# Rebuilding the order of all engines' instructions with measured times of small operations, in a four-layer attention kernel

## The chip, the cores and the metric

One NeuronCore of a Trainium2 chip. The metric is the device time of one execution in microseconds (us). Where a ratio is given, it is the mean time of one kernel's fast runs over the mean of the other's fast runs of the same rounds, with a 95% interval; it is therefore not quite the ratio of the medians that stand beside it.

## The reference, cut to what matters

Four residual layers on a sequence of 2048 rows of 512, 32 heads of 16:

```python
x = A_x
x = x + _A_ref(_layernorm(x), A_wqkv, A_w_phi, A_wo)   # linear attention
x = x + _B_ref(_layernorm(x), B_wqkv, B_wo)            # windowed attention
x = x + _A_ref(_layernorm(x), A_wqkv, A_w_phi, A_wo)
x = x + _B_ref(_layernorm(x), B_wqkv, B_wo)
# A: phi = softmax(q @ w_phi), softmax(-q @ w_phi); kv = sum over ALL rows of phi_k v; o = phi_q kv / (phi_q z)
# B: each row attends to rows i, i-2, ..., i-14 of its own head
```

The sum over all rows in A is what divides the run: nothing of A's output can start before all four row blocks have given their part. These are the two barriers of the text.

## The kernel before

The kernel is written as work items in threads ("stage.engine"). A list of 1452 entries replays them in one global order, so this list sets the order in which the instructions of all five engines stand in the program. Two more tables go with it: for each of 383 copies, residual adds and the like, whether Vector or Scalar does it, and for each buffer that is taken, which slot it gets.

```python
    def slot(self, kind):                       # which buffer
        k = self.ntile[kind]
        self.ntile[kind] = k + 1
        return kind + _SLOTS[kind][k]
    # ... cut ...
    def flex(self, stage, fn, *args):           # Vector ("1") or Scalar
        k = self.nflex
        self.nflex += 1
        self.step(stage, "F%d%s" % (k, fn.__name__), fn, *args, _CHOICE[k] == "1")
    # ... cut ...
    def run(self):
        self.setup()
        self.stages()                           # makes the threads
        n, left = {}, None
        for w in _ORDER.split():                # replays them
            key = self.names[int(w, 36)]
            i = n.get(key, 0)
            n[key] = i + 1
            self.threads[key][i]()
            if key == "flag.DVE" and i == 1:
                left = _OPT["flag_lag"]         # 12: the flag is read 12 entries later
            if left is not None:
                left -= 1
                if left == 0:
                    self.redo = self.flag()     # all engines read the flag (safe path or not)
        # ... cut ...
```

## Time and profile before

| | before |
|---|---|
| time, median of 3 | 333.4 us (332.74, 333.40, 334.26) |
| time of the profiled execution | 331.28 us (span in the trace 329.5) |
| busy Tensor, Vector, Scalar | 311.5, 302.7, 279.2 us |
| start to barrier 1, barrier 1 to 2, to the end of the last windowed product, from there to the end | 52.6, 157.2, 110.1, 9.6 us |

The lines behind the busy times are in the prediction. Barrier 1 is the start of the first `kvT` copy, barrier 2 the start of the second layer pair's `ZM` product, in all tables below.

### The profile page before, as it was taken

To read this page: it belongs to the slowest core of one execution; us is meant where nothing else is said; L and a number is where in the kernel's file an instruction comes from. 1 tells how busy PE (TensorE), PEld (TensorE's weight loads), DVE (VectorE), ACT (ScalarE), POOL (GpSimd) and SP (SyncE) were. 2 spreads that over 40 slices of the span, in tenths; PEclk is the share of its full clock that TensorE was granted. 3 is DMA by queue.
4 is the path that set the end of the run, shared out by engine and by line. 5 is a ranking of instruction groups with operands and counts; after the bars stand their busy time and mean duration, and the time that the engine had idled before them with its cause. 6 is when DMAs were issued, how large, how long until landed. Compare 5 with 4: busy or idle time off the path is not lost.

```text
span 329.5 us, 8061 instructions
## 1 busy us (share of the span) xinstructions
PE 311.5 (95%) x3203; PEld 149.7 (45%) x3203; DVE 302.7 (92%) x443; ACT 279.2 (85%) x634; POOL 26.9 (8%) x50
## 2 busy tenths in 40 slices
PE   8999999999999999899999999789999999997892
PEld 3645456435444454344443464543554444442330
DVE  8999994988999999899999999699999999999992
ACT  4999997999988979799999999699997887766550
POOL 4000000000040004000000000000004042400000
PEclk9999999999999999999999999999999999999998
DMA  7990000013757699994670300023359969799733
GB/s 200 313 252 6 0 2 4 2 47 92 127 141 152 143 156 138 139 157 98 114 148 4 64 3 2 4 69 90 116 72 190 133 130 147 138 150 160 161 115 120
DMA packets 37389, 35.42 MB, mean 107 GB/s; under 512 B 23008, under 2 KB 32224, under 8 KB 37344
## 3 DMA queue, kind: packets, MB, share of 16 engines
q1 hardware_dynamic: 36816, 34.81, 54.4%
q8 instruction: 27, 0.44, 0.7%
q14 instruction: 18, 0.15, 0.2%
q10 hardware_dynamic: 528, 0.02, 0.1%
HBM read 10.50 MB, written 2.36 MB: 39 GB/s over the span
## 4 chain that ended last, share of the span: by engine, by line
PE 60%; ACT 13%; DMA 12%; DVE 7%; SPq 3%; issue 2%; ACTq 0%; DVEq 0%
PE ps L893 18%; PE ps L516 9%; DMA Vg<-V 7%; PE ps L601 6%; PE ps L589 6%; PE ps L694 5%; DMA xnT<-xn 4%; PE ps L981 3%; ACT Ek L595 3%; ACT Eq L702 3%; PE ps L1045 2%; SPq L945 2%; DVE Eq L812 2%; PE ps L456 2%; ACT sqd L536 2%
## 5 line engine op out<-in xcount | busy, mean ns | idle before, releaser
L893 PE MATMUL ps<-xnT,WB 128*128 128x512 bf16 x384 | 88.4, 380 | 0.8 <-DMA xnT<-xn 0.8
L1036 DVE TENSOR_TENSOR pav<-PT,Vg 128x4096 bf16<-128x4096 bf16 (+1 forms) x34 | 71.8, 2162 | 1.9 <-DMA Vg<-V 1.2
L974 DVE TENSOR_TENSOR prod<-QT,K 128x4096 bf16<-128x4096 bf16 x32 | 72.2, 2285 | 0.5 <-ACT K L189 0.3
L893 PEld LDWEIGHTS <-WB 128*128 128x128 bf16 x384 | 42.3, 114 | 44.1 <-issue 7.6
L516 PEld LDWEIGHTS <-oT 128*128 128x128 bf16 x256 | 23.6, 98 | 33.6 <-ACT oT L189 4.3
L189 ACT CAST oT<-ps 128x512 bf16<-128x512 f32 (+1 forms) x55 | 29.5, 584 | 8.1 <-PE ps L1045 7.7
L702 ACT ACTIVATE Eq<-ps 128x512 bf16<-128x512 f32 x64 | 34.6, 617 | 1.3 <-PE ps L694 1.3
L595 ACT ACTIVATE Ek<-ps 128x512 bf16<-128x512 f32 x64 | 33.8, 612 | 0.8 <-PE ps L589 0.8
L516 PE MATMUL ps<-WoB,oT 128*128 128x512 bf16 x128 | 32.8, 380 | 0.3 <-ACT oT L189 0.2
L516 PE MATMUL ps<-WoA,oT 128*128 128x512 bf16 x128 | 30.9, 380 | 0.8 <-DVE oT L187 0.8
L694 PE MATMUL ps<-xnT,WA 128*128 128x512 bf16 x128 | 31.3, 380 | 0.2 <-DVE Eq L812 0.2
L536 ACT ACTIVATE sqd<-x 128x512 bf16<-128x512 bf16 x48 | 29.9, 629 | 1.3 <-DVE x L529 1.1
L601 PE MATMUL ps<-WA,xnT 128*128 128x512 bf16 x128 | 30.6, 379 | 0.0
L589 PE MATMUL ps<-WA,xnT 128*128 128x512 bf16 x128 | 30.4, 379 | 0.0
L529 DVE SCALAR_TENSOR_TENSOR x<-ps,x 128x512 bf16<-128x512 f32 x38 | 24.9, 684 | 1.4 <-PE ps L516 1.3
L189 ACT CAST K<-ps 128x512 bf16<-128x512 f32 x32 | 18.7, 591 | 3.6 <-PE ps L893 3.3
L189 ACT CAST QT<-ps 128x512 bf16<-128x512 f32 x31 | 18.2, 600 | 3.0 <-PE ps L893 3.0
L1045 PE MATMUL ps<-pav,indAV 128*32 128x512 bf16 (+1 forms) x272 | 17.5, 370 | 3.3 <-DVE pav L1036 2.9
L935 POOL COPY vh<-V 128x64 bf16<-128x64 bf16 x6 | 7.5, 1244 | 161.7 <-ACT V L189 161.7
L526 ACT ACTIVATE x<-ps 128x512 bf16<-128x512 f32 x26 | 15.1, 593 | 6.2 <-PE ps L519 5.7
L601 PEld LDWEIGHTS <-xnT 128*128 128x128 bf16 x128 | 12.3, 98 | 14.7 <-issue 0.4
L589 PEld LDWEIGHTS <-xnT 128*128 128x128 bf16 x128 | 12.3, 98 | 14.6 <-ACT xnT L189 0.4
(127 smaller groups left out, 451.1 us busy)
## 6 DMA issues: line engine op xcount, KB each, us to landing
Vg<-V SPq DMA_DIRECT2D x128, 131.5 KB, 4.5
Prho<-rd SPq DMA_DIRECT2D x8, 512.0 KB
x<-in_A_x_dram SPq DMA_DIRECT2D x3, 512.0 KB, 7.2
WB<-in_B_wqkv_dram SPq DMA_DIRECT2D x3, 512.0 KB, 8.9
wraw<-in_A_wqkv_dram SPq DMA_DIRECT2D x4, 256.0 KB, 4.5
out_dram<-x SPq DMA_DIRECT2D x4, 256.0 KB, 2.2
out_dram<-x SPq DMA_DIRECT2D x8, 128.0 KB, 2.5
x<-in_A_x_dram SPq DMA_DIRECT2D x4, 128.0 KB
```

Source lines behind the costliest of these rows:

```text
L189: self.nc.scalar.copy(out=out, in_=in_)
L516: nc.tensor.matmul(y[:], lhsT=oT[:, c, t * P:(t + 1) * P], rhs=Wo()[:, c, :], start=(c == 0), stop=(c == NB - 1 and not onpe))
L529: nc.vector.scalar_tensor_tensor(out=xb[:, t, :], in0=T[t][:], scalar=1.0, in1=xb[:, t, :], op0=ALU.mult, op1=ALU.add, **kw)
L536: nc.scalar.activation(out=sqd[:], in_=xb[:, t, :], func=ACT.Square, accum_out=T["ss"][:, t:t + 1])
L589: nc.tensor.matmul(pk[:], lhsT=xnT[:, t, k, :], rhs=self.WA[:, k, D:2 * D], start=(k == 0), stop=(k == NB - 1))
L595: nc.scalar.activation(out=T["E"][:, t, s, :], in_=T["k", t][:], func=ACT.Exp, scale=1.0 - 2.0 * s)
L601: nc.tensor.matmul(pv[:], lhsT=xnT[:, t, k, :], rhs=self.WA[:, k, 2 * D:3 * D], start=(k == 0), stop=(k == NB - 1))
L694: nc.tensor.matmul(pq[:], lhsT=self.WA[:, k, hb * P:(hb + 1) * P], rhs=xnT[:, :, k, :], start=(k == 0), stop=(k == NB - 1))
L702: nc.scalar.activation(out=self.Eq[L, b][s][:, :, hb, :], in_=T[hb][:].rearrange("p (t i) -> p t i", t=4), func=ACT.Exp, scale=1.0 - 2.0 * s)
L893: nc.tensor.matmul(pp[:], lhsT=self.WB[:, k, i * D + c:(i + 1) * D:NB], rhs=xnT[:, :, k, :], start=(k == 0), stop=(k == NB - 1))
L974: nc.vector.tensor_tensor(out=pr[:], in0=QT[:, c:c + 1, :].to_broadcast([P, NW, TB]), in1=win, op=ALU.mult)
L1036: nc.vector.tensor_tensor(out=pv, in0=PT[:, :, lo:lo + n].unsqueeze(1).to_broadcast([P, NB, 2, n]), in1=vw, op=ALU.mult)
```

## The change

Its intent: the three tables are planned anew, now with the measured times of small Vector and Scalar operations. New options come in as well, all off. Only the tables differ in what is emitted; core of the diff:

```diff
 _ORDER = """
-9 d6 b6 8 e a c 0 0 d i i i 0 0 i i i f h i i i i i i i i g j k o p j l 3 1x 1y t 3 1x t u m b o q r 34 1z s t
+av 8 i i i i i i i i i i i i 0 f 0 g e 2t 0 bs 9 h a d c 0 j k t i i j l 27 o p 3 3 d6 b 1x 1x t 1y o m 2 2 1q
 ... (all 1452 entries in a new order)
 _CHOICE = ( ... )     (86 of 383 flipped)
 _SLOTS = { ... }      (all four kinds new)
+    "v_dram": (), "half_mo": (), "rho_pad": 0,      (in the options; off, their code emits what was emitted)
```

## The prediction

> **What bounds the kernel now.** I read four views of the kernel before, in this order: the busy line of the page, the groups by line, Vector's waits in stretches of time, and the timelines of Tensor and Vector about the places where both lose time.
>
> The busy line and the slices, page parts 1 and 2 (busy tenths in 40 slices of 8.2 us):
>
> ```profile
> PE 311.5 (95%) x3203; PEld 149.7 (45%) x3203; DVE 302.7 (92%) x443; ACT 279.2 (85%) x634; POOL 26.9 (8%) x50
> ...
> PE   8999999999999999899999999789999999997892
> DVE  8999994988999999899999999699999999999992
> ```
>
> Three engines are nearly full at once. The span is 329.5 us, so Vector has 26.8 us in which it does nothing (329.5 - 302.7), and that includes the first 2 us and the end. It dips at slices 6 and 7 (about 50 to 57 us) and at slice 25 (about 206 to 214 us). These are the two barriers: the sums over keys of an A layer need all four row blocks, and nothing of the attention output can start before. Between row blocks, layers overlap, so there is other work at every other time.
>
> The costliest groups (line, engine, operation, shapes, count | busy us, mean ns | idle before):
>
> ```profile
> L893 PE MATMUL ps<-xnT,WB 128*128 128x512 bf16 x384 | 88.4, 380 | 0.8 <-DMA xnT<-xn 0.8
> L1036 DVE TENSOR_TENSOR pav<-PT,Vg 128x4096 bf16<-128x4096 bf16 (+1 forms) x34 | 71.8, 2162 | 1.9 <-DMA Vg<-V 1.2
> L974 DVE TENSOR_TENSOR prod<-QT,K 128x4096 bf16<-128x4096 bf16 x32 | 72.2, 2285 | 0.5 <-ACT K L189 0.3
> ```
>
> 144 of Vector's 302.7 us are 66 large products of the windowed layer that no order can shorten, and the idle time before them is 2.4 us in all. Little is lost inside the big work.
>
> Vector's named waits, from the list of waits of the whole run (us in total, times, longest):
>
> ```profile
> DVE ZM L749 <- PE ps L740: 2.4, 2, 1.8
> DVE kvT L187 <- PE ps L664: 2.0, 1, 2.0
> DVE rho L797 <- ACT Ds L793: 1.6, 2, 0.8
> DVE pav L1036 <- DMA Vg<-V: 1.2, 1, 1.2
> ```
>
> The first three are the two barriers and the short chain of small operations behind each. The largest other named wait is 1.2 us. So there is no single hole for a new order to fill.
>
> Tensor's timeline just before the first barrier:
>
> ```profile
> 50.49 2.04 PE L664 MATMUL ps<-Ek,vaug 128*33 128x64 bf16 x128
> 52.47 1.04 PE L694 MATMUL ps<-xnT,WA 128*128 128x512 bf16 x4
> ```
>
> From 7.2 to 52.5 us the chain that ended last is Tensor nearly without a break. Four matmuls of 512 columns take 0.86 us there, 215 ns each, against the 380 ns that the page gives as the duration of one: starts overlap, so I count Tensor by 215 ns. Priced so, Tensor has 20.1 us of issue in 20 to 40 us and 20.1 in 40 to 60: full. In 120 to 140 it has 17.1, in 200 to 220 it has 15.2, and in 300 to 329.5 about 18. So **Tensor bounds the start up to the first barrier**, Vector, Scalar and Tensor take turns between the barriers, and **Vector bounds the last 100 us** (20.00 of 20 us busy in 280 to 300).
>
> **What the Trainium skill says.** "VectorE: DVE Perf Modes", section "The TRN2 errata", gives (N+151)/0.96 ns for a Vector tensor_tensor at one element a cycle: 161 ns for 4 elements, 691 for 512. The trace agrees: 157 to 163 ns for the 128x4 statistics, 684 for the residual adds. The same table gives Scalar 224 cycles plus one an element at 1.2 GHz: 190 ns for 4 elements, and the trace has 206 for the 128x4 Exp but 296 for the 128x4 Ln; here the measurement decides. So small operations are nearly all fixed cost, and a planner that takes them for free is off by 0.2 to 0.3 us at each. "Perfetto Trace Analysis", section "Identifying the Most-Contended Engine", says that matmul busy share is no measure of nearness to the roofline; the 380 against 215 ns above agrees, and is why I do not read 95% as 5% of slack. Its section "Optimization Strategy" advises to go by regimes and to look for the gaps on the engine that binds in each; that is how I split the sum.
>
> **The change part by part.** The new options (values through memory, split output product, a padded row) are off, so their code emits what was emitted before. What differs is the order list, the choice of Vector or Scalar for 383 copies, residual adds and the like, and the slots of the buffers. The listing of the built programs shows the same number of instructions for Tensor, DMA issue and GpSimd. No product is made smaller.
>
> Of the choices, 86 flip. Pricing them by the groups (copy of 128x512 out of PSUM: Vector 0.686, Scalar 0.60; layer-norm apply: 0.408 and 0.808; 128x1024 transposed copy: 0.682 and 1.03; residual with its accumulator: 0.77 and 0.68; a product that reads PSUM itself 0.680, or 0.416 behind a Scalar copy of 0.60):
> - before the first barrier, to Vector: 3 applies, 3 transposed copies, 2 others; to Scalar: 2 applies, 7 copies. Vector -1.24 us, Scalar -0.08.
> - the rest of the first two layers: Vector +0.59, Scalar -1.33.
> - the last two layers: Vector -0.48, Scalar +1.13.
> - sum: Vector -1.1 us of 302.7, Scalar -0.3 of 279.2, Tensor 0.
>
> What of it lies on the path:
> 1. Start to first barrier: Tensor is full and its list before the barrier holds the same units in both (the transpose of the sums is at the same place). The 1.24 us that Vector saves become a longer wait, 0 us gained. Some Tensor units trade places, +-0.5.
> 2. First barrier to second: Scalar carries the chain in about 140 to 149 and 188 to 206 us, and loses 1.33 us of work; Vector gains 0.59. I credit half of the difference, -0.4 us. Of about 6 us of Vector's idle time here I let a better plan take a fifth, -1.2. This fifth is a choice; nothing in the listing proves it.
> 3. Second barrier: before, both late copies of V stood ahead of the last normalization (206.78 us). Now one stands behind it on Vector, 0.69 us, and the last key sums need it. +0.4.
> 4. Second barrier to the end: Vector-bound, -0.48 us of work, counted whole: -0.5. The lists of the last 20 us end alike (last product in halves, two projections, two residual adds, stores), so the 10 us from the last Vector product (ends 319.8) to the end stay: 0.
> Sum: -1.7 us. From 333.4 that is 331.7; I put **331.5**, since the order was presumably kept for looking better to its planner.
>
> **The rivals.**
> - *The better plan pays fully.* If right prices let the planner close half of Vector's removable idle time (26.8 less about 2 at the start and 8 at the end, so 17) the gain is 8 us, 325 us. For it: many small operations, 48 accumulator reads of 197 ns on Scalar alone. Against: the largest single wait outside the barriers is 1.2 us, and idle time at barriers is a chain of latencies, not order.
> - *Order moves the wait.* The windowed layer waits for gathered V at 126 to 135 us, with the DMA engines at 1.06 of their share in 120 to 140. The order of those transfers is unchanged in the first two layers, so saved Vector time ahead of it would only lengthen that wait. In the last two layers one more of row block 2's four gathers now stands behind those of row block 3; if it is late, Vector idles up to one landing time, 4.5 us (the page's median). That would make 334 to 337.
> - *Scalar becomes the bound in 222 to 260 us*, where it has 18.7 and 17.5 of 20 us and takes 1.13 us more. It would cancel step 4: 332 to 333.
>
> **Range and chances.** The planned terms sum to a couple of us. Errors: about 2 us from the idle time that I guessed in step 2, 1.5 from steps 1 and 3, 1 from spread of runs (before: 332.74 to 334.26). Together about 3: 8 in 10 between 327.5 and 335.0. Faster by over 2% means under 326.7, a gain of 6.7 us, 40% of the removable idle time: 0.08. Slower by over 2% means over 340: 0.03. Within 2%: 0.89.
>
> **What would show it right or wrong.** Step 1: the end of the first key sums stays within 0.7 us of 52.5, and Vector's wait for it is longer than 2.0 us. Step 2: Vector's idle time from 62 us to the second barrier falls by 1 to 2 us. Step 3: the second barrier's kvT evacuation comes within 2 us of 208.7, with the wait for it not shorter. Step 4: from there to the end 120.8 us becomes about 120. Busy sums: Vector 301.6, Scalar 279, Tensor issue unchanged. It is wrong if a wait for gathered V of over 2 us shows up on Vector, if Tensor stalls before the first barrier, or if the idle time between the barriers shrinks by 4 us or more.

## More of the kernel before

In four of the A layers' eight row blocks (2 and 3 of each layer) the reciprocal sums `rho` go through memory, so that they come back spread over all partitions; Vector multiplies the features by what comes back:

```python
        def wr():
            # ... cut ...
            nc.sync.dma_start(out=dst, in_=T["rho"][:])
        def rdb(s):                              # s = 0, 1: two reads of 512 KB
            T["P", s] = pr = self.med([4, NB, P], "Prho")
            # ... cut ...
            nc.sync.dma_start(out=pr[:].rearrange("p t a i -> p (t a i)"), in_=src)
        def muld(s):                             # Vector's product with it
            ev = self.Eq[L, b][s]
            nc.vector.tensor_tensor(out=ev[:], in0=ev[:], in1=T["P", s][:], op=ALU.mult)
```

And the output of a layer, whose residual add is a choice too:

```python
        def res(t, onpe):                        # "1": Tensor adds by an identity matmul, Scalar evacuates
            # ... cut ...
            if onpe:
                nc.scalar.activation(out=xb[:, t, :], in_=T[t][:], func=ACT.Identity, **kw)
            else:                                # "0": Vector adds
                nc.vector.scalar_tensor_tensor(out=xb[:, t, :], in0=T[t][:], scalar=1.0, in1=xb[:, t, :], ...)
        # ... cut ...
        def store(lo, hi):
            ov = self.out.rearrange("b (j p) d -> p (b j) d", p=P)
            nc.sync.dma_start(out=ov[:, 4 * b + lo:4 * b + hi, :], in_=xb[:, lo:hi, :])
```

## The result, and the profile after

| | before | after |
|---|---|---|
| time, median of 4 each | 333.07 us (332.54 to 334.26) | 329.17 us (328.77 to 330.32) |
| ratio of the means | | 0.9884 [0.9846, 0.9921] |
| busy Tensor, Vector, Scalar | 311.5, 302.7, 279.2 | 310.3, 302.2, 279.3 |

The time lies in the range and in the class that was given the best chance (within 2%), but the gain is 3.9 us and 1.7 had been added up. Run again in five rounds (controls below) it was 2.8 us, 0.9915 [0.9888, 0.9943].

The page of the kernel after, parts 1 and 2 (busy times; busy tenths in 40 slices):

```profile
PE 310.3 (95%) x3176; PEld 149.5 (46%) x3203; DVE 302.2 (92%) x439; ACT 279.3 (85%) x634; POOL 25.3 (8%) x50
...
PE   7999999999999999999999999979999999999873
...
DVE  7998995998998999899999999699999999999993
```

The busy times hardly move; the dips at the barriers stay. So most of what was gained is idle time: Vector's is 26.8 us before (329.5 - 302.7) and 25.3 after (327.5 - 302.2). Vector's named waits in the kernel after (us in total, times, longest):

```profile
DVE ZM L753 <- PE ps L744: 2.4, 2, 1.9
...
DVE rho L801 <- ACT Ds L797: 1.6, 2, 0.8
...
DVE pav L1081 <- DMA Vg<-V: 1.0, 1, 1.0
...
DVE kvT L190 <- PE ps L668: 0.7, 1, 0.7
```

The barrier waits are as before, but for the one at barrier 1 (2.0 before, 0.7 after), and no wait for gathered V has grown. To find where the gain is, the run was cut in four at the same events in each trace. Columns of this view are: stretch and length, then busy time (and instructions) of Tensor, weight load, Vector, Scalar, GpSimd, then clock, DMA share, GB/s. The kernel before, from its start to barrier 1, from 9.4 us after barrier 1 to barrier 2, from there to the last windowed product, and the tail:

```profile
0.00:52.58 52.58, 51.12 (x584) 28.20 (x585) 47.81 (x105) 46.60 (x97) 5.21 (x30) 1.00 0.44 122
62.00:209.81 147.81, 145.55 (x1459) 69.29 (x1458) 138.27 (x187) 137.10 (x321) 8.11 (x11) 1.00 0.54 96
209.81:319.91 110.10, 102.96 (x982) 46.76 (x983) 106.37 (x125) 86.85 (x199) 13.58 (x9) 1.00 0.68 121
319.91:329.50 9.59, 3.17 (x22) 1.18 (x20) 3.29 (x12) 0.61 (x2) 0.00 (x0) 0.84 0.46 149
```

The kernel after, the same stretches:

```profile
0.00:52.44 52.44, 50.36 (x579) 28.11 (x585) 47.04 (x104) 46.30 (x98) 5.12 (x30) 1.00 0.42 122
61.90:209.28 147.38, 145.02 (x1447) 68.94 (x1459) 139.16 (x188) 136.70 (x320) 7.27 (x11) 1.00 0.56 97
209.28:318.93 109.65, 102.56 (x973) 46.86 (x982) 106.14 (x126) 87.30 (x199) 12.91 (x9) 1.00 0.65 126
318.93:327.50 8.57, 3.23 (x22) 1.03 (x19) 3.04 (x7) 0.49 (x2) 0.00 (x0) 0.94 0.31 103
```

In this pair of traces the largest part (1.0 us of 2.0) is the tail, to which the prediction had given zero; between the barriers 0.4 us. But the pair explains 2.0 us and the timed runs differ by 3.9, so the profile of the kernel before is hardly of a usual run. That is what the experiments had to find out.

### The profile page after: what moved, and what is told of

It is laid out like the page before. It is cut to its first block, busy times and chain, and to the rows that moved or that the text cites. A ratio compares the mean times of both kernels' runs of the same rounds, so it can differ in the third digit from the quotient of the medians.

```text
span 327.5 us, 8033 instructions
## 1 busy us (share of the span) xinstructions
PE 310.3 (95%) x3176; PEld 149.5 (46%) x3203; DVE 302.2 (92%) x439; ACT 279.3 (85%) x634; POOL 25.3 (8%) x50
## 5 line engine op out<-in xcount | busy, mean ns | idle before, releaser
L192 ACT CAST oT<-ps 128x512 bf16<-128x512 f32 (+1 forms) x60 | 32.1, 587 | 8.4 <-PE ps L1090 7.1
L605 PE MATMUL ps<-WA,xnT 128*128 128x512 bf16 x120 | 30.0, 380 | 0.5 <-issue 0.2
L593 PE MATMUL ps<-WA,xnT 128*128 128x512 bf16 x124 | 29.7, 380 | 0.6 <-DMA xnT<-xn 0.2
L520 PE MATMUL ps<-WoA,oT 128*128 128x512 bf16 x120 | 29.2, 380 | 0.4
L192 ACT CAST V<-ps 128x512 bf16<-128x512 f32 x31 | 17.5, 595 | 4.4 <-PE ps L927 4.3
L192 ACT CAST K<-ps 128x512 bf16<-128x512 f32 x31 | 17.8, 585 | 3.7 <-PE ps L927 3.3
L192 ACT CAST QT<-ps 128x512 bf16<-128x512 f32 x29 | 17.1, 592 | 2.5 <-PE ps L927 2.5
L651 DVE TENSOR_TENSOR Ek<-Ek,rk 128x4096 bf16<-128x4096 bf16 (+1 forms) x10 | 18.6, 1858 | 0.5 <-ACT rk L646 0.5
L593 PEld LDWEIGHTS <-xnT 128*128 128x128 bf16 x128 | 12.1, 97 | 15.4 <-DMA xnT<-xn 0.7
L446 ACT ACTIVATE xn<-x,nmr,rstd 128x512 bf16<-128x512 bf16 x23 | 18.2, 822 | 1.0 <-DVE nmr L435 0.8
```

The costliest lines, as they stand in the source:

```text
L192: self.nc.scalar.copy(out=out, in_=in_)
L520: nc.tensor.matmul(y[:], lhsT=oT[:, c, t * P:(t + 1) * P], rhs=Wo()[:, c, :], start=(c == 0), stop=(c == NB - 1 and not onpe))
L593: nc.tensor.matmul(pk[:], lhsT=xnT[:, t, k, :], rhs=self.WA[:, k, D:2 * D], start=(k == 0), stop=(k == NB - 1))
L605: nc.tensor.matmul(pv[:], lhsT=xnT[:, t, k, :], rhs=self.WA[:, k, 2 * D:3 * D], start=(k == 0), stop=(k == NB - 1))
```

## The experiments

The record marks all variants as correct; even the one that is wrong on purpose passed the check. Twelve kernels ran, three calls of four, each on one chip with eleven runs of the kernel before; each kernel was run six times. By the author's account, five more variants did not build: the list with an item moved and the old slot table deadlocks, since a slot is then asked for before its holder is done. The traces' stretches, in us:

| kernel (first half / second half of the list) | to barrier 1 | barrier 1 to 2 | to last product | tail |
|---|---|---|---|---|
| before (profiled execution 331.28) | 52.58 | 157.23 | 110.10 | 9.59 |
| control of before (333.02) | 53.35 | 158.82 | 109.60 | 9.43 |
| after (329.18) | 52.44 | 156.84 | 109.65 | 8.57 |
| control of after (330.05) | 53.32 | 156.87 | 109.64 | 8.47 |
| after / before, cut at barrier 2 (331.90) | 53.11 | 156.70 | 111.14 | 9.15 |
| before / after, cut at barrier 2 (332.74) | 53.78 | 158.79 | 109.64 | 8.79 |
| before, one store earlier (332.56) | 52.83 | 158.92 | 109.85 | 9.20 |
| before, other factor in one product | 52.97 | 157.22 | 109.29 | 9.22 |
| after, one store later | 52.39 | 157.05 | 109.64 | 9.42 |

### Controls and grafts: which half carries it

The two kernels again under new names, and two grafts. At entry 985 of both lists, which is barrier 2, the same items have been done, so the lists can be joined there:

```diff
-order, choices, slots of one kernel
+first 985 entries of one kernel, the rest of the other; choices and slots go with their items
```

> The kernel before itself, run as a null control. Both theories: ratio 1.000 within 0.4%. It also gives a second trace: if the last Vector product again ends near 319.9 us and the span near 329.5 us, the profiled run of before was typical; the timed runs (332.5 to 334.3) against the profiled one (331.3) suggest instead a span of 330.5 to 332 us.

> The changed kernel again, for a tight size of the effect. Expected 0.988, interval within 0.984 to 0.992. Its trace should repeat: second barrier (first ZM product) at 209.3 us, last Vector product ended at 318.9, last residual add at 322.9, span 327.5.

> Changed order, choices and slots up to the second barrier, where both orders have done exactly the same work, and those of before from there on. Theory 1 (the gain comes late: Vector-bound second half and the tail; the traces show the second barrier only 0.5 us earlier): gain of 0.3 to 1.2 us, ratio 0.996 to 0.999. Theory 2 (the gain comes from the first two layers, and the profiled run of before was lucky there): ratio about 0.990 to 0.993, with the second barrier 2 us or more before that of the control.

> Order, choices and slots of before up to the second barrier, the changed ones from there on. Theory 1: most of the gain, ratio 0.989 to 0.994, the span after the second barrier 118.2 us as in the changed kernel (before 119.7). Theory 2: ratio 0.996 to 1.000.

| | median, us (lowest to highest) | ratio to before |
|---|---|---|
| control of before | 332.30 (330.59 to 333.30) | 0.998 [0.9947, 1.0013] |
| control of after | 329.81 (329.05 to 330.53) | 0.9915 [0.9888, 0.9943] |
| after, then before (graft_AB) | 330.79 (329.94 to 331.90) | 0.9943 [0.9915, 0.9970] |
| before, then after (graft_BA) | 330.92 (329.43 to 332.74) | 0.9942 [0.9912, 0.9971] |
| before, 11 runs | 332.82 (330.78 to 333.37) | |

Each half by itself gains about 0.6%, the whole 0.85%: neither carries it all, and the intervals are too wide to divide it. So neither theory held alone: the graft with the new first half reached barrier 2 2.4 us before the control (209.81 and 212.17 us), as theory 2 had it, and the other one kept about two thirds of the gain, just outside theory 1's range. (The profiled execution of the latter is the slowest of its six; its trace is only 0.2 us shorter than the control's, so most of its gain is not in that trace. The graft with the old second half is 1.3 us longer to its last product than the other traces of that half, 111.14 against 109.3 to 110.1, so a part of what it lacks may be the seam.) The start is the same for all (52.4 to 53.8 with no regard to the list), so by the traces the first half's part lies between the barriers, and the second half's is mostly the tail. Between the barriers the stretch takes two values with the old list, 157.2 and 158.8, and one with the new, 156.7 to 156.9. The control of before shows what the first profile did not. Vector's timeline of that control near 96 us (start, duration, line, operation, tiles; in brackets the idle time ahead of it and what ended it):

```profile
96.31 1.22 DVE L829 TENSOR_TENSOR Eq<-Eq,Prho 128x2048 bf16<-128x2048 bf16 x1
97.77 0.16 DVE L431 SCALAR_TENSOR_TENSOR nmr<-sums,rstd 128x4 f32<-128x4 f32 x1 [0.24 <-ACT rstd L427]
97.97 0.41 DVE L440 TENSOR_SCALAR xn<-x,rstd,nmr 128x512 bf16<-128x512 bf16 x1
100.34 1.23 DVE L829 TENSOR_TENSOR Eq<-Eq,Prho 128x2048 bf16<-128x2048 bf16 x1 [1.95 <-DMA Prho<-rd]
```

Vector stands 1.95 us for the second read of rho, that of row block 3 (counted from 0) of the first A layer; two of the expectations name the block or the layer wrongly. In the first profile of before this product ran at 97.40 us without a wait. With the old first half, three of four traces have the wait (1.95, 1.97, and 1.14 with another 1.10 beside it in the graft); the three that have it were executions of 332.56 to 333.02 us, the one without took 331.28. The timed runs of before fall into the same two groups: of 33, eight are at 331.62 or below and 25 at 331.94 or above, a gap of only 0.3 us between the groups. With the new first half no trace has it:

```profile
96.03 2.39 DVE L835 TENSOR_TENSOR Eq<-Eq,Prho 128x2048 bf16<-128x2048 bf16 x2
98.33 0.15 DVE L435 SCALAR_TENSOR_TENSOR nmr<-sums,rstd 128x4 f32<-128x4 f32 x1
```

Here (kernel after) both products run one behind the other. How the read is issued shows in Sync's queue of transfers (SPq: start and duration of the issue; `xnT` is a layer's transposed input, `Vg` the V that is gathered for the windowed layer). The control of before:

```profile
84.51 0.57 SPq L825 DMA_DIRECT2D Prho<-rd  x1
85.85 4.40 SPq L447 DMA_TRANSPOSE xnT<-xn  x1
90.35 0.60 SPq L825 DMA_DIRECT2D Prho<-rd  x1
94.50 8.39 SPq L945 DMA_DIRECT2D Vg<-V  x8
```

The kernel after:

```profile
83.10 0.57 SPq L831 DMA_DIRECT2D Prho<-rd  x1
87.06 3.03 SPq L451 DMA_TRANSPOSE xnT<-xn  x1
90.19 0.60 SPq L831 DMA_DIRECT2D Prho<-rd  x1
95.28 6.79 SPq L988 DMA_DIRECT2D Vg<-V  x8
```

In both the second read stands behind a transpose. The difference shows in the records of single packets, which tell rho reads (4096 B), transposes (256 B) and gathers (4208 B) apart:

```
                     read 1          transpose (bulk)  read 2          product starts
before               85.10 -  88.89   88.53 -  90.91   90.86 -  95.58    97.40
control of before    85.87 -  89.82   89.48 -  92.93   91.73 -  99.39   100.34
before, store moved  85.34 -  89.34   89.03 -  92.43   91.26 -  98.88    99.85
before / after       86.30 -  90.38   90.15 -  93.61   92.37 -  99.95   100.8
after                84.45 -  88.44   88.35 -  91.03   91.57 -  95.59    97.2
control of after     85.35 -  89.30   89.22 -  91.92   92.31 -  96.33    98.1
```

With the old list the second read starts before the transpose is through. In the three bad traces the two overlap for 1.2 us, but hardly move in it: the last 15 to 29 of the transpose's 2048 packets start there and 11 to 14 of the read's 128. The rest of the read follows, takes 7.6 us in all in place of 4.7, and its end falls among the gathers of V. With the new list the transpose is issued later (4.0 us after the first read in the kernel after, 1.3 us in the control of before), its issue is shorter (3.03 against 4.4 us), the read starts 0.4 to 0.5 us after the transpose has ended and takes 4.0 us in each trace. The lists agree with this: the transpose stands 2 entries behind the first read in the old one and 25 in the new one. And the packets show a difference in every trace of the two lists: with the old one some 260 packets of the transpose start while the first read still runs, with the new one none does. Whether this is what makes the second read late is not shown, for no run moved the transpose alone; why a transpose with the old list takes now 2.4 and now 3.4 us is not settled. Two further traces with the old first half (the other factor and the other slots, below) are of the early kind, so by the traces it is three of six, not three of four.

### Taking the wait away in the kernel before

```diff
-            nc.vector.tensor_tensor(out=ev[:], in0=ev[:], in1=T["P", s][:], op=ALU.mult)
+            p = self.Eq[L, b][0] if (L, b, s) == (0, 3, 1) else T["P", s]  # wrong on purpose
+            nc.vector.tensor_tensor(out=ev[:], in0=ev[:], in1=p[:], op=ALU.mult)
```

> Wrong on purpose. The kernel before, where Vector's product with the second read of rho in the third row block of the first layer takes another tile of the same shape (one that has long been there) as its factor. No instruction moves, the reads stay, only the wait of that product for the transfer goes. Theory 1 (the new order gains mainly because this wait, 2.0 us in three of four traces of the old order, is gone): barrier 1 to barrier 2 is 157.0 to 157.4 us, and the time falls by 1.0 to 1.6 us on the mean, to 331.0 to 331.6, all runs under 332; ratio 0.995 to 0.997. Theory 2 (the wait only stands for another that takes its place): segment 158 to 159 us, ratio 0.999 to 1.001.

Measured: 331.19 us (330.43 to 331.77, all under 332), ratio 0.9961 [0.9931, 0.9991]; barrier 1 to 2 took 157.22 us. The product of this variant, at the same place:

```profile
97.47 0.41 DVE L440 TENSOR_SCALAR xn<-x,rstd,nmr 128x512 bf16<-128x512 bf16 x1
97.80 1.22 DVE L830 TENSOR_TENSOR Eq<-Eq 128x2048 bf16<-128x2048 bf16 x1
98.93 0.68 DVE L187 CAST QT<-ps 128x512 bf16<-128x512 f32 x1
```

Every number came as theory 1 had it. But the trace proves nothing here: in this execution the read had landed by 95.79 us, so the product at 97.80 would not have waited for it in any case, as in the first trace of before (157.23 us). The proof is in the timed runs: all six are at 331.77 us or below, and of before's eleven beside them two are. So the wait for this one transfer is shown to cost the old list 1.3 us on the mean (0.4% of 333), and the slow group of runs goes with it; in a run that has it, it costs 1.6 us by the traces with and without it (158.82 and 157.22).

### Reading rho earlier in the kernel before

The obvious mend is the other way round: the second read directly behind the first, ahead of the transpose. Scalar's bound square (a check of the weights), whose buffer the read takes, had to go elsewhere and into another slot. The expectation says that it went earlier; the edit puts it later, from entry 471 to 545, and it ran at 114.38 us where it had run at 87.16:

```diff
 a3_03.SP#1   rdb(0)
+a3_03.SP#2   rdb(1)
 a4_01o.SP#0  transpose of row block 1
 ...
-a3_03.SP#2   rdb(1)
-bound.ACT#0  (slot 2 of "med")
+bound.ACT#0  (right behind entry 545, slot c)
```

> The kernel before with the second read of rho in the third layer issued directly behind the first, ahead of the transpose, and Scalar's bound square put earlier into another buffer so that the read's buffer is free. Theory 1 (half of the gain between the barriers is this read, which lands late in some runs): Vector's product with it waits for no transfer, barrier 1 to barrier 2 is 157.0 to 157.4 us where the kernel before had 157.2 and 158.8, and the time falls by 0.7 to 1.6 us, ratio 0.995 to 0.998. Theory 2 (the wait only hides another one that comes next): the segment stays at 158 to 159 us in the profile, ratio 0.999 to 1.001.

Measured: 341.74 us (340.69 to 342.86), ratio 1.0272 [1.0241, 1.0303]. Neither theory had this. The product waits for no read now, but Sync's queue and Tensor show the price:

```profile
84.01 1.56 SPq L825 DMA_DIRECT2D Prho<-rd  x2
85.74 8.28 SPq L447 DMA_TRANSPOSE xnT<-xn  x1
94.13 15.96 SPq L945 DMA_DIRECT2D Vg<-V  x8
...
98.59 9.61 PE L893 MATMUL ps<-xnT,WB 128*128 128x512 bf16 x32 [5.64 <-DMA xnT<-xn]
```

By the packets, both reads ran from 85.36 to 93.61 us and the bulk of the transpose from 93.32 to 97.64: the transpose moved nearly nothing until the reads ahead of it were done, and its issue held Sync for 8.28 us. Tensor then stood 5.6 us and Vector 7.9. So the transpose, not the read, is what the chain hangs on. The planner, old or new, does well to have it ahead of the second read. The run was confounded in one respect: the bound square was moved too, and that move was not run alone.

### The choices alone, the order alone

```diff
 before's order and slots, before's choices
-_CHOICE = before's
+_CHOICE = after's          (and the reverse in the kernel after)
```

> The kernel before with its own order and buffers, and the new kernel's choices between Vector and Scalar (86 flips). If the gain comes of the choices (Vector's work is 1.1 us less, Scalar's 0.3): ratio 0.992 to 0.997. If it comes of the order: ratio 0.999 to 1.005, since 86 flips meet an order that was planned for others.

> The new kernel's order and buffers with the choices of the kernel before. If the gain comes of the choices: ratio 0.997 to 1.002 against the kernel before. If it comes of the order: ratio 0.989 to 0.993, as the new kernel itself (0.988 and 0.9915), or up to 0.995 if the order needs its own choices.

Measured: 373.50 us (372.0 to 376.84), ratio 1.1245 [1.12, 1.1291], and 362.54 us (361.36 to 363.9), ratio 1.0902 [1.0866, 1.0938]. Both theories were far off. The busy times of Vector (303.2 and 304.3 us) are as ever. The old order with new choices, Vector's longest sums of waits (the first was 1.3 us in 5 waits with its own choices):

```profile
DVE x L529 <- PE ps L516: 19.5, 13, 5.7
DVE xnT L187 <- PE ps L456: 7.5, 2, 5.4
```

The new order with old choices:

```profile
DVE q L552 <- ACT sqd L540: 6.4, 8, 1.2
DVE x L533 <- PE ps L520: 5.9, 11, 1.3
DVE Eq L816 <- ACT bs L846: 5.3, 4, 2.1
```

A residual add that goes to Vector lands in Vector's queue at the place that had been planned for Scalar, ahead of its matmul's end, and everything behind it waits. Here an order and its choices are one plan; pricing the 86 flips by themselves (1.1 us of Vector) says nothing of what a flip does in its place.

### The slots alone

```diff
-_SLOTS = the plan's
+_SLOTS = at each request, the slot that has been out of use longest in the list
```

> The new kernel with its own order and choices, every buffer slot given instead to the one that has been out of use longest. If the planned slots carry part of the gain: 0.3 to 2 us slower than the new kernel, ratio 0.992 to 0.997 against the kernel before. If slots only have to be free in time: as the new kernel, 0.989 to 0.992.

> The kernel before with its own order and choices, every buffer slot given instead to the one that has been out of use longest. If the old slots cost it the gain (the second read of rho goes into a buffer that Scalar's bound square frees late): read issued or landed earlier, no wait of Vector for it, ratio 0.993 to 0.997. If slots only have to be free in time: ratio 0.999 to 1.001 and the wait is still there in the profile.

Measured: the new kernel 335.84 us (335.04 to 335.88), ratio 1.0093 [1.0063, 1.0123], against 0.9915 for its control; the old one 333.59 (333.01 to 334.63), ratio 1.0035 [1.0004, 1.0067]. So the new list loses 1.8%, about 6 us, with slots that look fair. 4.7 of them lie between the barriers (161.6 against 156.9 us), and Vector's longest new wait there is

```profile
99.89 0.16 DVE L552 TENSOR_TENSOR q<-q,ss 128x4 f32<-128x4 f32 x1 [2.03 <-ACT sqd L540]
```

in which Scalar is late because of its bound square:

```profile
95.40 1.91 ACT L413 ACTIVATE sq<-WA 128x2048 bf16<-128x2048 bf16 x1 [3.86 <-DMA xnT<-xn]
```

The square reads only weights. The new slot table gives it the buffer of the tile that the transpose reads, so here the slot itself is the wait; the planned table gives it another, and the kernel after has no such wait. The guess that slots only have to be free in time is wrong for the new list; "longest out of use" in the list is not "longest out of use" in time. For the old list the run is no test of its theory: the slot rule gave the second read of rho the same buffer as before, again behind the bound square. That its trace has no wait for rho says nothing, as the first trace of before has none either. Which other slots matter was not tried.

### The tail: one store earlier, one store later

The tail differed by the place of a 256 KB store (rows 2 and 3 of row block 1), which the old list holds back to the third last place.

```diff
 before, one store earlier:            after, one store later:
+b3_11o.SP#1  store(2, 4)              -b3_11o.SP#1  store(2, 4)
 b3_13o.SP#0                            b3_13o.SP#0
 ...                                    ...
 b3_12o.SP#0, #1                        b3_12o.SP#0, #1
-b3_11o.SP#1  store(2, 4)              +b3_11o.SP#1  store(2, 4)
 b3_12o.SP#2, #3                        b3_12o.SP#2, #3
```

> The kernel before with one token moved: the store of the second half of row block 1 goes out where its data are ready (about 308 us) instead of among the last four stores. Theory 1 (the tail is shorter in the new kernel because that store no longer stands in the queue of the last ones): from the end of the last windowed product to the end of the span 9.4 us becomes 8.4 to 8.8, and the time is 0.7 to 1.1 us less, ratio 0.997 to 0.998. Theory 2 (the tail is shorter because of what Tensor and Scalar do there): the tail stays at 9.2 to 9.6 us, ratio 1.000.

> The new kernel with the store of the second half of row block 1 put back among the last four stores, as in the kernel before. Theory 1 (that store among the last ones costs the whole 1 us of the tail): from the end of the last windowed product to the end 8.5 us becomes 9.4, ratio 0.993 to 0.995 against the kernel before. Theory 2 (it costs 0.2 to 0.3 us, as the run with it moved in the kernel before suggests, and the rest of the tail is another thing): 8.6 to 8.9 us, ratio 0.990 to 0.992.

Measured: before with the store earlier 332.53 us (331.39 to 332.87), ratio 0.999 [0.9962, 1.0018], tail 9.20 us. After with the store later 330.47 us (329.48 to 333.71), ratio 0.9948 [0.9904, 0.9992], tail 9.42 us against 8.57 and 8.47. The times alone separate neither from its parent; the traces say more. Sync's own records of the last stores, with the end of Vector's last residual add beside them (us):

```
                       last add ends   last store starts   its data are in   end of span
before                    323.80         324.20               327.12          329.50
before, store earlier     325.49         325.52               328.33          330.78
after                     322.91         322.94               324.97          327.46
control of after          323.81         323.84               325.95          328.33
after, store later        323.07         324.53               326.13          328.48
Sync, before:      323.09 store | 323.47 to 324.07 read of the flag | 324.20 last store
Sync, after:       321.61 to 322.15 read of the flag | 322.28 store | 322.94 last store
Sync, store later: 322.38 the 256 KB store | 322.86 store, 1.57 us to issue | 324.53 last store
```

From the data to the end of the span it is 2.35 to 2.5 us in all of them. Ahead of that there are two things. In the kernel before, Sync's read of the flag (0.60 us) falls between the last two stores and delays the last by 0.37 us; it is emitted 12 list entries behind the flag, and that is ahead of the last of the four stores in the old list and ahead of the last two in the new one, where the last store starts 0.03 us behind its data. Moving the store out of the old list also shifted that count by one, and the read went behind the last store: this, not the store, is the 0.37 us that the variant shows. The rest is the landing of the last store, 2.9 us with the old list (2.8 even with the store moved) and 2.0 to 2.1 with the new in the table. The other traces blur this: with the old second half it is 2.4 (graft), 2.5 (other factor) and 2.8 us (control), and with the new second half behind the old first one it is 2.4. Over all of them the tail is 9.15 to 9.59 us with the old second half and 8.47 to 8.79 with the new, 0.7 us apart on the mean. Theory 1 thus fails for the old list: the store there is not what makes the tail long. In the new list the same store put back does go with the 0.9 us of theory 1, through an issue that holds Sync for 1.57 us; that the store ahead causes this long issue is likely and not shown, for the last stores of the kernel after and its control took 0.78 and 1.06 us to issue with no such store just ahead. So part of the tail's gain is shown to be the place of the flag's read (0.37 us); the rest, 0.4 to 0.6 us, is measured and without a shown cause.

## Why the prediction was right or wrong

**The sum.** With the wait in about three runs of four (read from the two groups of timed runs; the count is an inference), the traces give: start 0; barrier 1 to 2, 1.6 x 0.75 = 1.2 for the wait and 0.35 beside it (157.22 to 156.87); barrier 2 to last product 0.1 (mean of the four uncut old traces 109.7, new 109.6); tail 1.0 (0.7 over all traces). Together 2.6 us, against 2.8 between the eleven runs of before and the control of after (means 332.63 and 329.80) and 3.9 in the first comparison of four runs each. The prediction had 1.2 (steps 2 and 3), 0.5 and 0 for the last three.

The time fell within a range of 7.5 us that the prediction gave 8 in 10. One reading of lines was off: Vector's tenths dip in one slice at the first barrier (slice 6 from 0, a 4), not in two. Its 161 and 190 ns for 4 elements are estimates from the two formulas that it cites, and the Exp and the Ln that it sets beside the second are two forms: in the code the Ln has a bias tile (`eps_t`), the Exp has none.

**Step 1** was right in its time: barrier 1 came at 52.44 us, within 0.7 of 52.5, and nothing was gained up to it. The saved work was also real, 47.81 to 47.04 us of Vector, 0.77 and not 1.24. The check that its wait there would grow beyond 2.0 us was wrong: it shrank to 0.7. Vector's idle time before the barrier did grow, from 4.77 to 5.40 us, but elsewhere; a saved instruction leaves its gap where the engine next has to wait, which need not be the last wait of the stretch.

**Step 2** had about the right size by luck, for the wrong reason. It let a better plan take "a fifth" of about 6 us of Vector's idle time (9.54 us in the trace, with the wait at barrier 2), and Vector's idle time from 62 us to barrier 2 fell by 1.3 us against the first trace (9.54 to 8.22) and 3.0 against the control's. The work moved as forecast in sign only: Vector +0.89 and Scalar -0.40 us in this stretch, where +0.59 and -1.33 had been added up. The runs showed no general tightening; they showed one wait for a transfer of which the only profile had nothing, because it was of an execution from the faster quarter. The step that failed was to take that profile for the usual run when its time, 331.28 us, stood outside the timed ones.

**Step 3**, 0.4 us lost at barrier 2 to a V copy behind the last normalization, did not come. The two trade places: before, the copy (206.01) and then the normalization (206.78 us); after, the normalization (205.59) and then the copy (206.73). From the end of the later one to the barrier it is 1.80 and 1.86 us, so the copy had been on the path before as well. The step counted an exchange as a loss. Its check half held: the `kvT` copy came at 208.21 us, within 2 us of 208.7, but the wait for it was shorter (0.71 us, 1.03 before).

**Step 4** had Vector's stretch at 0.5 us and it was 0.1, for Vector's saved work there is 0.23 us (106.37 to 106.14). The tail, "the lists of the last 20 us end alike, so ... stay: 0", was the mis-sized term: 1.0 us. The lists do end alike for Tensor and Vector; what differs is Sync's, a read of the flag and the issue and landing of stores, and these had not been looked at because Sync is never counted busy.

**The rivals.** That a better plan pays fully (325 us) was wrong, and so was that the wait for gathered V grows: 1.0 and 1.1 us in the two traces of the kernel after, 1.2 before. Scalar did get fuller where the rival had it, 19.11 of 20 us in 240 to 260 (17.45 before) beside Vector's 19.31, but the stretch from barrier 2 to the last product grew no longer (109.65 and 110.10 us). Not among the rivals was what the swaps show: that a table taken from elsewhere with the others fixed costs up to 12%, so the term "86 flips, 1.1 us of Vector" had no meaning taken alone, though it happened to be small.

## What to carry to other kernels

Compare the profiled execution's own time with the timed runs before reading it; if it lies outside them, the trace may lack something that the usual run has, and a second trace is worth more than a finer reading of the first. In this kernel an order list, its engine choices and its buffer slots were one plan, and no piece of it could be judged alone: of the edits here to one piece, only the one that took out a wait altogether gained, and the others cost between nothing and 12%. When the end of a run matters, read the issuing engine's own records, not only the busy ones: a register read between the last two stores cost 0.37 us, more than all of Vector's work that the change saved in the last hundred microseconds (0.23).

## What the Trainium skill lacked or had wrong

- "DMA: Bandwidth & Descriptors", section "DMA Transpose (X-bar)", gives no figure for how long the issue of a transpose holds the issuing engine when other transfers stand ahead of it on the queue. Here it held Sync 2.9 to 4.6 us with one 512 KB read ahead and 8.28 us with two, where the whole kernel lost 2.7%; the other transposes of the kernels before and after took 1.7 to 3.0 us each. The bulk of its packets moved only when the reads were done. That the transpose is held by the reads themselves and not by something that goes with them was not tested by itself.
- "Advanced Engine Details and Errata", section "X-Bar Transpose (TRN2)", expects 350-400 GB/s. The 512 KB transpose here took 2.7 us for its 2048 packets of 256 B in the kernel after, some 195 GB/s, and up to 3.5 us where a rho read started before its last packets; it is, as the page says, no slower than a plain transfer: the rho read of the same size took 3.9 to 4.0 with nothing beside it (that read repeats rows from memory, so it is not the plainest of transfers).
- "DMA: Bandwidth & Descriptors", section "Issuing engines are not separate DMA queues", calls the time to initiate a DMA "usually small relative to the DMA itself". This agrees for most stores (0.33 to 0.45 us against a landing of about 2), but the last stores with the new list took 0.78 and 1.06 us to issue, and one took 1.57 us when a 256 KB store stood directly ahead of it, in a run whose tail was 0.9 us longer.
